# Moving transposes from the matmul engine to DMA in a sorted-attention kernel, with a paired value turn and a new order of the first item

## Chip, cores, metric

One core of one Trainium2 chip. The metric is device microseconds (us) of one execution; lower is better. Engines: PE is the matmul engine (TensorE), PEld its weight load, DVE is VectorE, ACT is ScalarE, POOL is GpSimd, SP issues DMAs.

## The reference

Four batch items, each with 8 heads, 768 positions and 64 dimensions per head, then one feed-forward layer on the joined heads. Inputs and output are float32; the kernel computes in bf16.

```python
def _attn_ref(q, k, v, sort_net):
    P = sort_net                       # (4, 8, 8, 8): per head an 8x8 matrix
    for _ in range(5):                 # exp, then rows and columns normalised
        P = np.exp(P - np.max(P, axis=-1, keepdims=True))
        P = P / (np.sum(P, axis=-1, keepdims=True) + 1e-09)
        P = P / (np.sum(P, axis=-2, keepdims=True) + 1e-09)
    # blocks of 96 positions are mixed by P ("sorted")
    k_sorted = np.einsum('bhij,bhjcd->bhicd', P, k_b)
    v_sorted = np.einsum('bhij,bhjcd->bhicd', P, v_b)
    # softmax attention inside each block: q block i with k_sorted, v_sorted block i
    ...
def _moe_ref(x, w1, w2, w_out):        # x: 3072 x 512, w1 and w2: 512 x 1024
    return np.maximum(x @ w1, x @ w2) @ w_out
```

Since max(h1, h2) = relu(h1 - h2) + h2, the kernel computes h with w1 - w2 ("w_difference") and adds x @ (w2 @ w_out) by a product "wc" formed once.

## The kernel before, in the parts that matter

PSUM is the memory in which PE leaves its results; an "eviction" is the copy out of it by ACT or DVE (1.01 and 1.22 us for 128x1024 elements), which frees the buffer. All PSUM tiles, whatever their name, come from one pool with four buffers.

```python
psum = ctx.enter_context(tc.tile_pool(name="psum", bufs=4, ...))
def ps_f32(name): return psum.tile([128, 1024], FP32, tag="ps", name=name)

def keep_streaming(ps, n, by=None):        # filler matmuls of zeros, n columns
    w0 = fill[:, 0:128] if by is None else late[by]
    while n > 0:
        w = min(n, 512)
        nc.tensor.matmul(ps[:, 0:w], w0, fill[:, 0:w], start=True, stop=True)
        n -= w

def turn_v(rows, eng, c0, c1):             # v from (position, dim) to (dim, position)
    dst = v_dc[rows, 0 : D * BLK].rearrange("p (d c) -> p d c", c=BLK)[:, :, c0:c1]
    src = v_raw[rows].rearrange("p (c d) -> p d c", d=D)[:, :, c0:c1]
    # ACT: nc.scalar.copy, DVE: nc.vector.tensor_copy

def q_transposes(b, half, eng=None):       # ... allocates qT[b] when half == 0
    ps = ps_bf16("tq_ps")
    for n in range(2 * R):                 # R = 6
        if b in q_pair:                    # two heads side by side: one matmul for both
            nc.tensor.matmul(ps[:, c], q_pair[b][:, hp, r], ident, is_transpose=True, ...)
            continue
        for h2 in range(2):                # else one matmul per head
            nc.tensor.matmul(ps[h2 * 64 : ..., c], q_raw[b][:, hp + 4 * h2, ...], ident,
                             is_transpose=True, ...)
    evac(qT[b][...], ps[...], ...)         # eviction on ACT or DVE

def sort_v(b, t, n=0, eng=None):           # 16 matmuls, weights from v_dc (dense columns)
    ps = ps_f32("v_ps")
    keep_streaming(ps, n)
    for m in range(16):
        d = t * 16 + m
        nc.tensor.matmul(..., v_dc[r0 : r0 + 64, d * BLK : d * BLK + 128], bd_v[b][...], ...)
    evac(...)

def x_transposes(b, t, eng=None):          # 8 matmuls and an eviction with re-ordering
    ps = ps_bf16("tx_ps")
    x = x_tiles.pop((b, ih, hh))
    for m in range(8): nc.tensor.matmul(..., is_transpose=True, ...)
    evac(xT[...], ps..., 2 * TCH, eng=eng)
```

While item b runs through the layer (its "units": eight h units of 1.3 us, then output products), the attention of item b + 1 is prepared between the units. The preparation is a list of **steps**. The loop spreads them evenly by their count. SC is a score group (PE, then an exponential on ACT), VA a values group, TR an x transpose, ks and vs key and value sorts, qs the two q transpose halves.

```python
for b in range(B):
    ...
    if b == 0:
        steps = group(*vs[:3]) + qs[:1] + group(*SC[0:2], vs[3]) + qs[1:] + VA[:1]
        steps += group(*SC[2:5]) + VA[1:2]
    elif b == 1: ...                        # pair_q, key sorts, q, scores, value sorts
    else: ...
    steps += VA[2:3] + TR[:1] + VA[3:4]
    steps += group(*rest[:-1]) + TR[1:2] + VA[4:5] + rest[-1:] + VA[5:6]
    done = 0
    for n, unit in enumerate(units):
        unit()
        for step in tail.get(n, []): step()          # fixed places
        total = sum(cost[lo:-2])
        want = -(-len(steps) * sum(cost[lo : n + 1]) // total)   # by count of steps
        while done < min(want, len(steps)):
            steps[done](); done += 1
    tail = {0: [VA[6]], 1: [TR[2], VA[7]], 2: [TR[3]]}
```

The softmax here doesn't subtract the row's maximum and nothing guards it: scores larger than these inputs give would overflow.

## Time and profile before

| | before |
|---|---|
| time, median of 4 runs | 181.78 us (181.24 to 182.06) |
| span of the profiled run | 179.5 us |
| PE busy | 170.0 us, 95% of the span |
| DVE, ACT busy | 94.0 us, 91.8 us |
| clock granted to PE | 1.00 |

The views that carry the argument (busy shares, stretches, chain, waits in the timeline) are quoted in the prediction. Three rows of the groups are added here. Their columns: line, engine, operation, output<-input, shapes, count, then total busy us and the mean ns of one, then idle time before.

```profile
L209 DVE COPY v_dc<-v_raw 64x1536 bf16<-64x1536 bf16 x4 | 5.8, 1492 | 0.0
L207 ACT COPY v_dc<-v_raw 64x1152 bf16<-64x1152 bf16 x1 | 2.2, 2158 | 0.0
L392 PEld LDWEIGHTS <-v_dc 64*128 64x128 bf16 x128 | 4.1, 95 | 1.1 <-issue 0.9
```

A turn of v costs 1492 ns on DVE for 1536 elements, 2158 ns on ACT for 1152; a value weight load costs 95 ns.

### The profile page before, as it was taken

Reading aid. Unit: us, or ns where it says so; the run is one execution under the profiler, and the core shown is the slowest. Engines: PE = TensorE matmul, PEld = TensorE weight load, DVE = VectorE, ACT = ScalarE, POOL = GpSimd, SP = SyncE. Lnnn points to the kernel's source line nnn. Section 1 sums busy time; section 2 is a strip of 40 time slices with the busy share of each in tenths; the row PEclk is TensorE's granted clock in tenths of the full one; section 3 lists DMA queues with packets and bytes.
Section 4 is the critical chain, followed back from the end, with each engine's and each line's share of the span. In section 5 each row is a group of like instructions: output and inputs, shape, how many; then the busy total and the mean of one; then the engine's idle time right before and its main releaser. Section 6 shows DMA issues by size and latency. Waiting matters only on the chain.

```text
span 179.5 us, 4648 instructions
## 1 busy us (share of the span) xinstructions
PE 170.0 (95%) x2083; PEld 100.7 (56%) x2083; DVE 94.0 (52%) x192; ACT 91.8 (51%) x110; POOL 22.9 (13%) x39
## 2 busy tenths in 40 slices
PE   7797989999999989999989999999999999999993
PEld 2246666666565535577655554657555546554453
DVE  5878498559864395253586436156245415340210
ACT  3695876777664445368784341465833233520021
POOL 7861443200180000001000000000000000000000
PEclk9999999999999999999999999999999999999999
DMA  3999999999299991235600113200001132000333
GB/s 58 201 204 206 200 207 214 194 202 208 55 120 221 206 250 48 99 117 74 108 4 0 57 63 117 104 17 5 0 4 42 74 117 116 4 0 4 117 117 117
DMA packets 13939, 19.17 MB, mean 107 GB/s; under 512 B 800, under 2 KB 8864, under 8 KB 13920
## 3 DMA queue, kind: packets, MB, share of 16 engines
q0 software_dynamic: 10304, 12.58, 41.6%
q1 hardware_dynamic: 3328, 6.10, 8.9%
q8 instruction: 16, 0.26, 0.6%
q10 hardware_dynamic: 288, 0.20, 0.3%
q14 instruction: 3, 0.02, 0.0%
HBM read 25.17 MB, written 6.29 MB: 175 GB/s over the span
## 4 chain that ended last, share of the span: by engine, by line
PE 58%; DMA 29%; DVE 5%; issue 4%; POOL 2%; ACT 1%; POOLq 0%; DVEq 0%
PE out_ps L590 32%; PE h_ps L563 16%; DMA v_raw<-in_v_dram 10%; DMA w_sb<-in_moe_w_dram 10%; DMA q_raw<-in_q_dram 9%; PE o_ps L463 3%; PE tx_ps L495 2%; PE k_ps L371 2%; PE s_ps L438 2%; DVE g L579 2%; PE tq_ps L341 1%; DVE x L480 1%; DVE xT L105 1%; POOL v_raw L153 1%; DVE v_dc L209 1%
## 5 line engine op out<-in xcount | busy, mean ns | idle before, releaser
L590 PE MATMUL out_ps<-wo_sb,g 128*128 128x512 bf16 (+2 forms) x208 | 48.1, 363 | 0.2 <-DVE g L579 0.2
L563 PE MATMUL h_ps<-xT,w_sb 128*128 128x384 bf16 x256 | 46.1, 326 | 0.5 <-DVE g L579 0.2
L563 PEld LDWEIGHTS <-w_sb 128*128 128x128 bf16 x256 | 23.6, 97 | 15.1 <-issue 0.7
L577 ACT ACTIVATE g<-h_ps 128x768 bf16<-128x768 f32 x24 | 19.4, 811 | 23.4 <-PE h_ps L563 23.4
L446 ACT ACTIVATE e<-s_ps 96x768 bf16<-96x768 f32 x32 | 24.1, 804 | 14.0 <-PE s_ps L438 13.9
L590 PEld LDWEIGHTS <-g 128*128 128x128 bf16 x208 | 17.7, 97 | 15.8 <-issue 0.2
L590 PE MATMUL out_ps<-wc,xT 128*128 128x512 bf16 (+2 forms) x104 | 25.0, 362 | 0.0
L103 ACT COPY o<-out_ps 128x1024 f32<-128x1024 f32 x8 | 8.1, 1012 | 31.0 <-PE out_ps L590 27.3
L480 DVE TENSOR_TENSOR x<-o_ps,rs 96x512 bf16<-96x512 f32 x32 | 22.0, 687 | 1.1
L474 DVE RECIPROCAL rs<-o_ps 96x8 f32<-96x8 f32 x32 | 6.4, 201 | 27.4 <-PE o_ps L463 27.2
L590 PEld LDWEIGHTS <-xT 128*128 128x128 bf16 x104 | 9.9, 98 | 10.9
L209 DVE COPY v_dc<-v_raw 64x1536 bf16<-64x1536 bf16 (+2 forms) x9 | 14.1, 1583 | 1.8 <-DMA v_raw<-in_v_dram 1.7
L463 PEld LDWEIGHTS <-e 96*128 96x128 bf16 x256 | 11.2, 98 | 6.5 <-DVE x L480 1.1
L579 DVE TENSOR_SCALAR g<-h_ps 128x768 bf16<-128x768 f32 x8 | 7.7, 958 | 13.5 <-PE h_ps L563 10.6
L463 PE MATMUL o_ps<-v_sb,e 96*128 96x65 bf16 x256 | 12.9, 193 | 1.3 <-DVE x L480 0.6
L105 DVE CAST v_sb<-v_ps 96x1024 bf16<-96x1024 f32 x7 | 8.5, 1217 | 5.9 <-PE v_ps L392 3.9
L103 ACT CAST v_sb<-v_ps 96x1024 bf16<-96x1024 f32 x9 | 8.7, 1010 | 3.4 <-PE v_ps L392 2.6
L103 ACT CAST kT<-k_ps 128x1024 bf16<-128x1024 f32 x10 | 9.5, 1024 | 0.0
L103 ACT COPY xT<-tx_ps 128x768 bf16<-128x768 bf16 x11 | 8.8, 797 | 1.5 <-PE tx_ps L495 1.5
L438 PEld LDWEIGHTS <-kT 64*128 64x128 bf16 x256 | 6.2, 94 | 5.4 <-issue 4.4
L129 POOL DMA_DIRECT2D q_raw<-in_q_dram x4 | 3.6, 901 | 43.0 <-DVE q_pair L326 40.7
L438 PE MATMUL s_ps<-qT,kT 64*128 64x96 bf16 x256 | 9.0, 204 | 0.1
(78 smaller groups left out, 162.5 us busy)
## 6 DMA issues: line engine op xcount, KB each, us to landing
out_dram<-o SPq DMA_DIRECT2D x11, 512.0 KB, 2.8
k_raw<-in_k_dram POOLq DMA_DIRECT2D x12, 256.0 KB, 13.7
q_raw<-in_q_dram POOLq DMA_DIRECT2D x4, 768.0 KB, 8.9
v_raw<-in_v_dram POOLq DMA_DIRECT2D x6, 384.0 KB, 12.0
w_sb<-in_moe_w_dram POOLq DMA_DIRECT2D x3, 512.0 KB, 15.7
wo_sb<-in_moe_w_out_dram POOLq DMA_DIRECT2D x2, 512.0 KB, 19.9
v_raw<-in_v_dram POOLq DMA_DIRECT2D x3, 256.0 KB, 5.1
w_sb<-in_moe_w_dram POOLq DMA_DIRECT2D x2, 256.0 KB, 14.3
```

What stands on the lines that cost most here:

```text
L103: nc.scalar.copy(out=out_ap, in_=in_ap)
L105: nc.vector.tensor_copy(out=out_ap, in_=in_ap)
L209: nc.vector.tensor_copy(out=dst, in_=src)
L438: nc.tensor.matmul(ps[:, h2 * 512 + ii * BLK : h2 * 512 + (ii + 1) * BLK], kT[b][rows, (hp * 8 + i) * BLK : (hp * 8 + i) * BLK + 128], rhs ...
L446: nc.scalar.activation(out=e[:, 0 : 8 * BLK].rearrange("p (t f) -> p t f", t=2), in_=ps[0:BLK].rearrange("p (t f) -> p t f", t=2)[:, :, 0 ...
L463: nc.tensor.matmul(ps[:, h2 * 512 + ii * 65 : h2 * 512 + (ii + 1) * 65], e[:, (h2 * 4 + ii) * BLK : (h2 * 4 + ii) * BLK + 128], v_sb[:, m0 ...
L474: nc.vector.reciprocal(out=rs, in_=ov[:, :, :, 64])
L480: nc.vector.tensor_tensor(out=x, in0=ov[:, :, :, 0:D], in1=rs.to_broadcast([BLK, 2, 4, D]), op=ALU.mult,)
L563: nc.tensor.matmul(h_ps[t][:, m * 512 : m * 512 + TCH], w1_sb[:, hp, fb * 128 : (fb + 1) * 128], xT[:, b % 2, ch, hp % 2, hp // 2, :], sta ...
L577: nc.scalar.activation(out=g, in_=src, func=AF.Relu)
L579: nc.vector.tensor_scalar(out=g, in0=src, scalar1=0.0, scalar2=None, op0=ALU.max)
L590: nc.tensor.matmul(dst, g_tiles[b, ch, m // 2][:, m % 2, off : off + 128] if m < NFB else xT[:, b % 2, ch, hp % 2, hp // 2, off : off + 12 ...
```

## The change

Its intent is to take work off PE, which sets the time after 40 us. The x transposes of items 2 to 4 and the q transposes of items 3 and 4 become DMA transposes; the q transposes of item 2 stay on PE and lose their pairing. The value turn moves pairs of bf16 as 32-bit words on DVE (and pair by pair on ACT), so that value weights are read with a step of two. The first item is put in another order with far fewer filler matmuls, the opening fillers have 160 columns instead of 512, and the loads are queued in another order. The step lists are adapted: more of each item's x transposes lie in them, and fewer in the fixed places. Not shown in the cut below: the re-ordering of positions moves from the eviction of x to the exponential, the scores take 128 columns each in PSUM, and x gets a fourth buffer.

```diff
-    keep_streaming(ps_f32("fill_ps"), 18 * 512)
+    keep_streaming(ps_f32("fill_ps"), 76 * 160, most=160)
 # turn_v on DVE; on ACT the same pairs as a fourth dimension "two"
+        out=dst.bitcast(U32).rearrange("p (d c) -> p d c", c=BLK)[:, :, c0:c1],
+        in_=src.bitcast(U32).rearrange("p (c d) -> p d c", c=BLK)[:, :, c0:c1],
+    def v_weights(rows, d):
+        c = d // 2 * (2 * BLK) + d % 2
+        return v_dc[rows, c : c + 255 : 2]
 # q_transposes; the paired form on PE goes
+        if b > 1:
+            nc.sync.dma_start_transpose(out=qT[b][:, hps]..., in_=q_pair[b][:, hps]...)
+            return
 # x_transposes
+        if b:
+            nc.sync.dma_start_transpose(out=xT[:, b % 2, ih, hh]..., in_=x...)
+            return
 # first item (cut): order changed, fillers thinned
-    sort_v(0, 0, 256, "A")
-    sort_v(0, 1, 384, "A")
+    sort_v(0, 0, 0, "D")
+    sort_v(0, 1, 0, "A")
 ... (cut: further lines of this kind)
-        8: [pair_q(1, 0), pair_q(1, 1), load_q(2), load_v(2), load_v(3)],
+        9: [load_v(2), load_v(3), load_k(3)],
+        14: [load_q(2)],
+        18: [pair_q(2, 0), pair_q(2, 1), load_q(3)],
             elif b == 1:
-                steps = group(*pairs) + group(*ks) + qs[:1] + group(*SC[0:2], vs[0]) + qs[1:]
-                steps += group(*vs[1:4]) + group(*vs[4:7]) + group(*SC[2:4], vs[7]) + VA[:2]
+                tail[1] = qs
+                steps = group(*ks) + group(*vs[0:3]) + group(*vs[3:6]) + group(*vs[6:8])
+                steps += group(*SC[0:2]) + group(*SC[2:4]) + VA[:2]
             else:
-                steps = group(*pairs) + group(*ks) + qs + group(*SC[0:2])
+                tail[1] = qs
+                tail[4] = ks
+                steps = group(*SC[0:2]) + group(*SC[2:5]) + VA[:2]
+                lo = 6
 # all items
             steps += group(*rest[:-1]) + TR[1:2] + VA[4:5] + rest[-1:] + VA[5:6]
+            steps += TR[2:3] + VA[6:7]
-        tail = {0: [VA[6]], 1: [TR[2], VA[7]], 2: [TR[3]]}
+        tail = {0: [VA[7], TR[3]]}
```

More of the change, by code (lines that the diff above doesn't have):

```diff
@@ L12 @@
 BF16 = mybir.dt.bfloat16
+U32 = mybir.dt.uint32
 @with_exitstack
@@ L74, with keep_streaming @@
     late = {}
-    def keep_streaming(ps, n, by=None):
+    def keep_streaming(ps, n, by=None, most=512):
         w0 = fill[:, 0:128] if by is None else late[by]
         while n > 0:
-            w = min(n, 512)
+            w = min(n, most)
             nc.tensor.matmul(ps[:, 0:w], w0, fill[:, 0:w], start=True, stop=True)
@@ L118 @@
         nc.vector.memset(kT[b][:, 32 * BLK :], 0.0)
-    v_dc = big.tile([128, D * BLK + 32], BF16, tag="v_dc", name="v_dc")
+    v_dc = big.tile([128, D * BLK + 64], BF16, tag="v_dc", name="v_dc")
     nc.vector.memset(v_dc[:, D * BLK :], 0.0)
@@ L203, in turn_v @@
     def turn_v(rows, eng, c0, c1):
-        dst = v_dc[rows, 0 : D * BLK].rearrange("p (d c) -> p d c", c=BLK)[:, :, c0:c1]
-        src = v_raw[rows].rearrange("p (c d) -> p d c", d=D)[:, :, c0:c1]
+        dst, src = v_dc[rows, 0 : D * BLK], v_raw[rows]
         if eng == "A":
-            nc.scalar.copy(out=dst, in_=src)
-        else:
-            nc.vector.tensor_copy(out=dst, in_=src)
+            nc.scalar.copy(
+                out=dst.rearrange("p (d c two) -> p d c two", c=BLK, two=2)[:, :, c0:c1],
+                in_=src.rearrange("p (c d two) -> p d c two", c=BLK, two=2)[:, :, c0:c1],
+            )
+        else:
+            nc.vector.tensor_copy(
+                out=dst.bitcast(U32).rearrange("p (d c) -> p d c", c=BLK)[:, :, c0:c1],
+                in_=src.bitcast(U32).rearrange("p (c d) -> p d c", c=BLK)[:, :, c0:c1],
+            )
+    def v_weights(rows, d):
+        c = d // 2 * (2 * BLK) + d % 2
+        return v_dc[rows, c : c + 255 : 2]
     rowsum = const.tile([G, NB], FP32, tag="rowsum", name="rowsum")
@@ L335, in q_transposes @@
             qT[b] = qpool.tile([128, HP, R, 128], BF16, tag="qT", name="qT")
+        if b > 1:
+            hps = slice(half * 2, half * 2 + 2)
+            nc.sync.dma_start_transpose(
+                out=qT[b][:, hps].rearrange("p h r c -> p (h r) c"),
+                in_=q_pair[b][:, hps].rearrange("p h r d -> p (h r d)"),
+            )
+            return
         ps = ps_bf16("tq_ps")
@@ L339, in q_transposes @@
             c = slice(n * 128, (n + 1) * 128)
-            if b in q_pair:
-                nc.tensor.matmul(
-                    ps[:, c], q_pair[b][:, hp, r], ident, is_transpose=True, start=True, stop=True
-                )
-                continue
             for h2 in range(2):
@@ L393, in sort_v @@
                 ps[:, m * 64 : (m + 1) * 64],
-                v_dc[r0 : r0 + 64, d * BLK : d * BLK + 128],
+                v_weights(slice(r0, r0 + 64), d),
                 bd_v[b][r0 : r0 + 64, :],
@@ L414, in sort_v_pair @@
                     ps[:, par * 512 + m * 64 : par * 512 + (m + 1) * 64],
-                    v_dc[rows, d * BLK : d * BLK + 128],
+                    v_weights(rows, d),
                     bd_v[b][rows, :],
@@ L438, in scores @@
                 nc.tensor.matmul(
-                    ps[:, h2 * 512 + ii * BLK : h2 * 512 + (ii + 1) * BLK],
+                    ps[:, h2 * 512 + ii * 128 : h2 * 512 + ii * 128 + BLK],
                     kT[b][rows, (hp * 8 + i) * BLK : (hp * 8 + i) * BLK + 128],
@@ L446, in scores @@
         nc.scalar.activation(
-            out=e[:, 0 : 8 * BLK].rearrange("p (t f) -> p t f", t=2),
-            in_=ps[0:BLK].rearrange("p (t f) -> p t f", t=2)[:, :, 0 : 4 * BLK],
+            out=e[:, 0 : 8 * BLK].rearrange("p (t c r) -> p t c r", t=8, r=R),
+            in_=ps[0:BLK]
+            .rearrange("p (t f) -> p t f", t=8)[:, :, 0:BLK]
+            .rearrange("p t (r c) -> p t c r", r=R),
             func=AF.Exp,
@@ L476, in values @@
             x_tiles[b, ih, hp // 2] = xpool.tile(
-                [BLK, 2, 4, 2, D], BF16, tag="x", name="x", bufs=3
+                [BLK, 2, 4, 2, D], BF16, tag="x", name="x", bufs=4
             )
@@ L490, in x_transposes @@
         ih, hh = divmod(t, 2)
+        x = x_tiles.pop((b, ih, hh))
+        if b:
+            nc.sync.dma_start_transpose(
+                out=xT[:, b % 2, ih, hh].rearrange("p h (i c) -> p (h i) c", c=BLK),
+                in_=x.rearrange("p t i n d -> p (t i n d)"),
+            )
+            return
         ps = ps_bf16("tx_ps")
-        x = x_tiles.pop((b, ih, hh))
         for m in range(8):
@@ L495, in x_transposes @@
             nc.tensor.matmul(
-                ps[:, h2 * 1024 + ii * BLK : h2 * 1024 + (ii + 1) * BLK],
+                ps[:, m * BLK : (m + 1) * BLK],
                 x[:, h2, ii].rearrange("p n d -> p (n d)"),
@@ L502, in x_transposes @@
             )
-        dst = xT[:, b % 2, ih, hh].rearrange("p h (i c r) -> p h i c r", r=R, c=PB)
-        src = ps.rearrange("p (h f) -> p h f", h=2)[:, :, 0:TCH].rearrange(
-            "p h (i r c) -> p h i c r", r=R, c=PB
+        evac(
+            xT[:, b % 2, ih, hh].rearrange("p h f -> p (h f)"),
+            ps[:, 0 : 2 * TCH],
+            2 * TCH,
+            two_x=True,
+            eng=eng,
         )
-        evac(dst, src, 2 * TCH, eng=eng)
     w2T = big.tile([128, NFB, DMODEL], BF16, tag="w2T", name="w2T")
@@ L647 @@
             selections(0)
-            turn_v(first, "A", 0, 11)
+            turn_v(first, "A", 0, 18)
         if it == 3:
-            turn_v(first, "A", 11, 22)
-    turn_v(first, "A", 22, 40)
+            turn_v(first, "A", 18, 36)
+    turn_v(first, "A", 36, 56)
+    turn_v(first, "A", 56, 80)
     block_diagonals(0)
-    turn_v(first, "D", 56, 96)
-    turn_v(first, "A", 40, 56)
+    turn_v(first, "D", 80, 96)
     SC, VA, TR = att(0)
     sort_k(0, 0, 2048, "A")
-    sort_k(0, 1, 512, "A")
-    sort_k(0, 2, 256, "D")
+    sort_k(0, 1, 256, "D")
+    sort_k(0, 2, 256, "A")
+    sort_v(0, 0, 0, "D")
+    sort_v(0, 1, 0, "A")
     q_transposes(0, 0, "D")
-    sort_v(0, 0, 256, "A")
-    sort_v(0, 1, 384, "A")
-    sort_v(0, 2, 384, "D")
-    sort_v(0, 3, 384, "A")
+    sort_v(0, 2, 0, "A")
+    scores(0, 0)
+    sort_v(0, 3, 0, "D")
+    scores(0, 1)
     q_transposes(0, 1, "D")
-    scores(0, 0, 256)
-    scores(0, 1, 256)
-    values(0, 0, 512)
+    values(0, 0)
     SC[2]()
+    VA[1]()
     SC[3]()
-    VA[1]()
-    values(0, 2, 512)
+    values(0, 2, 256)
     x_transposes(0, 0, "A")
@@ L675 @@
     SC[4]()
-    moe_h_products(0, 0, 0, (0, 2), 512)
+    moe_h_products(0, 0, 0, (0, 2), 256)
     x_transposes(0, 1, "A")
@@ L691, in turn @@
         turn_v(rows, "D", c0, c0 + 24)
-        load["D"] += 1600
+        load["D"] += 850
     def load_rest():
@@ L706 @@
         7: [lambda: turn(second, 72)],
-        8: [
-            lambda: pair_q(1, 0),
-            lambda: pair_q(1, 1),
-            lambda: load_q(2),
-            lambda: load_v(2),
-            lambda: load_v(3),
-        ],
+        9: [lambda: load_v(2), lambda: load_v(3), lambda: load_k(3)],
+        14: [lambda: load_q(2)],
+        18: [lambda: pair_q(2, 0), lambda: pair_q(2, 1), lambda: load_q(3)],
     }
@@ L738 @@
             qs = [lambda half=half: q_transposes(b + 1, half) for half in range(2)]
-            pairs = [lambda two=two: pair_q(b + 1, two) for two in range(2)]
             ks = [lambda t=t, b=b: sort_k(b + 1, t) for t in range(3)]
@@ L755 @@
                 vs = [lambda t=t: sort_v_pair(2, t) for t in range(8)]
-                steps = group(*pairs) + group(*ks) + qs[:1] + group(*SC[0:2], vs[0]) + qs[1:]
-                steps += group(*vs[1:4]) + group(*vs[4:7]) + group(*SC[2:4], vs[7]) + VA[:2]
-            else:
-                steps = group(*pairs) + group(*ks) + qs + group(*SC[0:2])
-                steps += group(*SC[2:5]) + VA[:2]
+                tail[1] = qs
+                tail[10] = [lambda: pair_q(3, 0), lambda: pair_q(3, 1)]
+                steps = group(*ks) + group(*vs[0:3]) + group(*vs[3:6]) + group(*vs[6:8])
+                steps += group(*SC[0:2]) + group(*SC[2:4]) + VA[:2]
+            else:
+                tail[1] = qs
+                tail[4] = ks
+                steps = group(*SC[0:2]) + group(*SC[2:5]) + VA[:2]
+                lo = 6
             rest = SC[4:] if b == 1 else SC[5:]
@@ L773 @@
                 done += 1
-        tail = {0: [VA[6]], 1: [TR[2], VA[7]], 2: [TR[3]]}
-        if b == 0:
-            tail[3] = [lambda: load_k(3)]
-            tail[8] = [lambda: load_q(3)]
+        tail = {0: [VA[7], TR[3]]}
 _INS = ['q', 'k', 'v', 'sort_net', 'moe_w1', 'moe_w2', 'moe_w_out']
```

## The prediction

> **What bounds the kernel now.** I read the page's busy shares first, then busy time by stretches, then the chain that ended last, then the timeline of its weak places.
>
> ```profile
> PE 170.0 (95%) x2083; PEld 100.7 (56%) x2083; DVE 94.0 (52%) x192; ACT 91.8 (51%) x110; POOL 22.9 (13%) x39
> ...
> 70.00:80.00 10.00, 10.00 (x87) 5.58 (x85) 4.78 (x10) 4.74 (x6) 0.00 (x0) 1.00 0.28 106
> 80.00:90.00 10.00, 9.85 (x197) 7.15 (x194) 4.97 (x7) 7.69 (x10) 0.90 (x1) 1.00 0.58 82
> ...
> 100.00:110.00 10.00, 10.00 (x101) 5.23 (x100) 4.10 (x7) 4.59 (x6) 0.00 (x0) 1.00 0.18 68
> ```
>
> In the stretches (start:end, length, then busy time of PE, weight loads, DVE, ACT and POOL, then clock, DMA share and GB/s) PE is full from about 40 us to 177 us, while DVE and ACT are half used. So from 40 us on, time on PE is time of the kernel, and DVE or ACT time is worth something only where PE waits for it. The chain gives what each kind of PE work costs there, overlap taken out:
>
> ```profile
> 80.38 0.34 PE tx_ps L495 x8
> 80.72 1.64 PE k_ps L371 x96
> 82.36 1.41 PE h_ps L563 x8
> 83.76 0.67 PE tq_ps L341 x12
> 84.43 1.31 PE h_ps L563 x8
> ```
>
> A group of eight x transposes costs 0.34 us and a half of an item's paired q transposes 0.67 us, though the groups list 0.2 us for each single matmul: those durations overlap. The waits that remain on PE after 40 us are few. Two, in the timeline:
>
> ```profile
> 64.39 0.42 PE L463 MATMUL o_ps<-v_sb,e 96*128 96x65 bf16 x8 [0.60 <-DVE x L480]
> ...
> 154.10 0.51 PE L495 MATMUL tx_ps<-ident,x 96*128 96x96 bf16 x8 [0.34 <-DVE x L480]
> ```
>
> The 0.60 us goes back to DVE idling 1.72 us for v_raw, whose load stood in the POOL queue behind a q load that waited for pair_q. The 0.34 us at 154 us is the end of an item, where the last x must be normalised before it is transposed; there is another such at 118.5 us. Waits for a PSUM buffer that DVE still evicts come to 0.24, 0.24 and 0.26 us (91, 94 and 130 us). In all about 2.0 us.
>
> Before 40 us the start is set by latencies and by the loads, which run at 200 GB/s or more in every slice to 45 us:
>
> ```profile
> 27.31 0.67 DVE L190 TENSOR_TENSOR w_sb<-w_sb 128x1024 bf16<-128x1024 bf16 x1
> 28.66 1.23 DVE L105 COPY w2T<-tw_ps 128x2048 bf16<-128x2048 bf16 x1 [0.68 <-PE tw_ps L518]
> 29.81 0.68 DVE L190 TENSOR_TENSOR w_sb<-w_sb 128x1024 bf16<-128x1024 bf16 x1
> ```
>
> The weight difference at 27.31 us starts just as the last w1 piece lands (27.17 us by the chain). That landing does not move with this change, so a faster attention before it is worth only what lies after it: the 0.68 us for which DVE then waits for PE.
>
> [...] The trace fits a cost by element: turns of 2560 and 1536 elements took 2.38 and 1.49 us, so 0.87 ns per element and 0.16 us fixed; 768 words should take 0.83 us. [...] The paired layout makes the value weights step by two; the present loads are all dense (16 loads with their matmuls in about 0.5 us), so no run here shows it yet. [...] The trace has no transposing DMA. Its plain 512 KB stores land 2.8 us after issue[...].
>
> **The change part by part.**
>
> x transposes of items 2 to 4 (b = 1 to 3) leave PE: 12 groups x 0.34 = 4.1 us off the path. Their evictions (about 0.8 us on ACT, 0.95 us on DVE, 12 of them, some 10 us) leave engines that are not the bound. Each becomes one DMA of 96x1024 bf16 = 197 KB[...].
>
> q transposes of items 3 and 4 leave PE: 4 x 0.67 = 2.7 us. Item 2 loses its pairing: 24 instructions instead of 12 per half. Unpaired, the next PE instruction starts 0.79 us later (20.00 to 20.79), paired 0.68 us (49.46 to 50.14), so +0.1 x 2 = +0.2 us. The DMA of a half is 393 KB[...]; they are issued after the second unit of an item and first used some 8 to 9 us later (five h units of 1.3 us plus the key sort of 1.64 us). [...]
>
> Load order: both value loads now stand ahead of the q load, and the first half of v_raw is free from 13 us on. They should land near 53 us in place of 61.9, ahead of the first two-item turn. That ends the 0.60 us wait.
>
> Paired turn: four turns of 1.48 us at 41 to 47 us and four of 1.48 us at 62 to 72 us become 0.83 us each: 5 us off DVE, none of it directly on the path; it helps the three buffer waits. On ACT the present turn costs (2158-1384)/(1152-704) = 1.73 ns per element, twice DVE's; if one access fetches a pair it becomes about 0.87, and 18 columns (1152 elements) take 1.2 us, inside the space of 1.6 us that ACT has between two exponentials.
>
> First item: without most of the filler matmuls, and with value sorts ahead of the q that arrives at 15.9 us, my replay of the new order with the old durations puts the first h product at 24.0 us in place of 25.9. Then DVE waits for the w1 piece at 27.2 us and goes on without a gap: difference 0.68, eviction 1.2, difference 0.68, normalising 0.9, so the third h unit at 30.8 us in place of 31.8. I take -0.8 us. The 160-column fillers at the beginning run longer, but end near 8.6 us, beside the normalisation steps that set the time until 11.3 us: no change.
>
> Item ends: the 0.34 us waits at 118 and 154 us go, as no PE transpose waits for x. In their place the first h unit of the second half (the fifth unit) waits for the last x's DMA. From the end of its values group there are three h units, 3.9 us, plus 0.3 us as the late half is used second; normalising takes 1.1 us of it. That leaves 3.1 us for a transfer[...]. For item 2 the last q load is in flight then, so I put 0.5 us of waiting there and 0.2 us for each of the other two.
>
> Third item's preparation: six sorts now follow one unit without an h unit between them, with four PSUM buffers. Evictions of about 1 us on two engines need some 7 us for 7.8 us of PE work. I allow 0.4 us of new waits and count the old buffer waits (0.7 us) as only half gone.
>
> Sum: -4.1 - 2.7 + 0.2 - 0.6 - 0.7 (item ends) - 0.35 - 0.8 + 0.9 + 0.4 = -7.8 us, so 174.0. The waits on DMA are the softest term; without them it is 172.7. I choose 173.6 us, 4.5% below 181.78.
>
> **The rivals.**
>
> First: the transposes by DMA are late. For it: [...]the issuing queue is shared in order with the output stores, and the last q load is in flight at the first item end. Against it: the DMA share falls to 0.14 to 0.28 from 100 us on, and the third x transposes of an item were moved earlier, as by someone who knows the latency. At 5 us each[...] it costs about 2 us at three item ends, and 1 to 2 us before the scores of items 3 and 4: 179 to 181 us.
>
> Second: strided value weights load slower. If a load takes twice as long, 128 loads after 40 us for the paired items and 64 for item 2 cost 15 to 30 ns more each, 3 to 4 us: 177 us. [...]
>
> Third: the transposes are hidden anyway, as PE work moved elsewhere. I give it little: the chain from 40 us on is PE from instruction to instruction, and DVE and ACT have half their time free, so no other engine takes over at once. It would leave only the start and the load order, 180 us.
>
> Fourth, upward: the head gains the whole 2 us (if the w1 piece is not what holds it) and no DMA is waited for: 171 us.
>
> **Range and chances.** The removed PE work, 6.8 us, is the firm part; the rivals can each take back 2 to 5 us, and I think neither likely nor both at once. Range 170.8 to 177.6 us. The 2% limit lies at 178.1 us, so faster 0.90, same 0.08, slower 0.02.
>
> **What would show it right or wrong.** Right: PE's instruction count falls by 96 + 48 and rises by 24 for the transposes (fillers apart), PE busy stays at 95% or above, the stretches from 40 us on stay full, no wait of PE for DMA exceeds 0.5 us, turns of 768 words take 0.83 us, and the third h unit begins near 30.8 us. Wrong: PE waiting for xT or qT behind a DMA, the value sorts taking over 0.5 us per 16, ACT turns above 1.6 us that hold up the exponentials, or DVE and ACT evictions showing up as releasers of PE in the third item's preparation. If issue to landing of an x transpose is above 3.1 us, my term for the item ends is too small.

## The result and the profile after

Ratios in this document are the mean time of one kernel's fast runs over the mean of the fast runs of the kernel before in the same rounds, so they are not quite the ratio of the medians quoted.

| | before | after |
|---|---|---|
| median of 4 runs | 181.78 us (181.24 to 182.06) | 178.19 us (176.69 to 179.71) |
| the runs of after | | 176.84, 179.54 (slow), 176.69, 179.71 (slow) |
| ratio of fast runs, 95% | | 0.972 (0.970 to 0.975) |
| span, profiled run (fast) | 179.5 us | 175.0 us |
| PE busy | 170.0 us | 162.3 us |

The change is faster, by 2.8% in its fast runs. Two of its four runs were slow, which the kernel before almost never shows (1 of 33 runs). This is a second finding beside the size of the gain; both are followed below. The first page line of after is this:

```profile
PE 162.3 (93%) x1999; PEld 99.8 (57%) x2014; DVE 83.1 (47%) x186; ACT 79.9 (46%) x98; POOL 22.9 (13%) x39
```

PE lost 7.7 us of busy time, DVE 10.9 and ACT 11.9. But the span lost only 4.5: PE's busy share *fell* from 95% to 93%. The groups that answer to those shown of before:

```profile
L212 DVE COPY v_dc<-v_raw 64x768 uint32<-64x768 uint32 x4 | 3.2, 834 | 0.0
L207 ACT COPY v_dc<-v_raw 64x1152 bf16<-64x1152 bf16 x2 | 2.4, 1176 | 0.0
L404 PEld LDWEIGHTS <-v_dc 64*128 64x128 bf16 x128 | 4.0, 95 | 0.6 <-issue 0.4
```

The turn went from 1492 to 834 ns on DVE, so a word takes about as long as a single bf16 element did, which the prediction had assumed and the trace of before does not show; on ACT it went from 2158 to 1176 ns (in pairs 1536 elements take 1511 ns, so 0.87 ns per element). A weight load with a step of two still takes 95 ns. The DMA issues (output<-input, issuing engine, count, then median us from issue to landing):

```profile
xT<-x SPq DMA_TRANSPOSE x12, 3.5
qT<-q_pair SPq DMA_TRANSPOSE x4, 4.1
```

The quickest x took 2.8 us for its 197 KB, the quickest q 3.6 us for 393 KB; the median of x is above the 3.1 us that the prediction had left for it at the item ends. The same three stretches as in the prediction:

```profile
70.00:80.00 10.00, 9.95 (x155) 6.04 (x153) 1.78 (x4) 4.01 (x5) 0.00 (x0) 1.00 1.11 205
80.00:90.00 10.00, 8.90 (x197) 5.73 (x192) 5.75 (x6) 8.64 (x11) 0.00 (x0) 1.00 0.63 100
...
100.00:110.00 10.00, 9.95 (x74) 4.88 (x74) 2.67 (x6) 2.95 (x4) 0.00 (x0) 1.00 0.52 144
```

From 80 to 90 us PE now stands for 1.1 us of ten. The waits of PE after 40 us (who waited <- for what: us in total, times, longest) say for what:

```profile
PE h_ps L585 <- DMA xT<-x: 0.8, 1, 0.8
PE out_ps L612 <- DVE o L106: 0.7, 1, 0.7
PE o_ps L477 <- ACT e L458: 0.6, 1, 0.6
PE out_ps L612 <- ACT o L104: 0.5, 1, 0.5
PE h_ps L585 <- ACT kT L104: 0.5, 1, 0.5
PE v_ps L425 <- ACT kT L104: 0.5, 1, 0.5
PE h_ps L585 <- ACT e L458: 0.4, 1, 0.4
...
```

Five more lines of 0.2 to 0.3 us follow. One wait is for a DMA (0.76 us). The others are 4.5 us together, of which 0.3 us are put down to issue. The remaining 4.2 us, nine waits, are of one kind: a PE group needs a PSUM buffer, and ACT or DVE has not yet emptied one. Before, waits of that kind were 0.74 us after 40 us, and all waits together about 2.0.

The spans can be cut at the same PE work in each timeline. "Paced" is an experiment described below; it differs from after only in the spreading of the steps.

| stretch of PE work | before | after | paced |
|---|---|---|---|
| start to the key sort of item 2 | 42.76 | 41.47 | 42.01 |
| to the first h product of item 2 | 32.72 | 32.75 | 31.79 |
| to the first h product of item 3 | 37.82 | 36.33 | 35.08 |
| to the first h product of item 4 | 35.56 | 33.76 | 32.34 |
| to the end | 30.65 | 30.72 | 30.72 |
| span | 179.51 | 175.03 | 171.94 |

In these traces the first item's new order gave 1.3 us, the stretches to the h products of items 3 and 4 gave 1.5 and 1.8; the second and the last stretch gave nothing. The first stretch is the least steady: paced leaves it as it is in after, and over six traces of that same start it is 41.21 to 42.01.

### The profile page after: what moved, and what is told of

It is laid out like the page before. It is cut to its first block, busy times and chain, and to the rows that moved or that the text cites. A ratio compares the mean times of both kernels' runs of the same rounds, so it can differ in the third digit from the quotient of the medians.

```text
span 175.0 us, 4519 instructions
## 1 busy us (share of the span) xinstructions
PE 162.3 (93%) x1999; PEld 99.8 (57%) x2014; DVE 83.1 (47%) x186; ACT 79.9 (46%) x98; POOL 22.9 (13%) x39
## 4 chain that ended last, share of the span: by engine, by line
PE 73%; DMA 9%; ACT 6%; issue 5%; DVE 2%; POOL 2%; ACTq 0%; DVEq 0%; POOLq 0%
PE out_ps L612 33%; PE h_ps L585 23%; DMA q_raw<-in_q_dram 7%; PE wc_ps L563 4%; PE o_ps L477 3%; PE k_ps L383 3%; ACT e L458 3%; PE s_ps L450 2%; DMA xT<-x 2%; ACT g L599 2%; PE tq_ps L358 1%; PE v_ps L404 1%; DVE qT L106 1%; PE tw_ps L540 1%; POOL k_raw L145 1%
## 5 line engine op out<-in xcount | busy, mean ns | idle before, releaser
L612 PE MATMUL out_ps<-wo_sb,g 128*128 128x512 bf16 (+2 forms) x198 | 46.2, 362 | 1.8 <-DVE o L106 0.7
L585 PE MATMUL h_ps<-xT,w_sb 128*128 128x384 bf16 x256 | 45.2, 326 | 1.9 <-DMA xT<-x 0.8
L599 ACT ACTIVATE g<-h_ps 128x768 bf16<-128x768 f32 x23 | 18.6, 812 | 18.1 <-PE h_ps L585 18.1
L601 DVE TENSOR_SCALAR g<-h_ps 128x768 bf16<-128x768 f32 x9 | 8.6, 957 | 18.2 <-PE h_ps L585 18.2
L612 PEld LDWEIGHTS <-xT 128*128 128x128 bf16 x104 | 9.9, 98 | 10.9
L106 DVE CAST v_sb<-v_ps 96x1024 bf16<-96x1024 f32 x8 | 9.7, 1217 | 8.0 <-PE v_ps L425 5.1
L104 ACT CAST kT<-k_ps 128x1024 bf16<-128x1024 f32 x9 | 8.8, 1016 | 3.0 <-PE k_ps L383 3.0
L104 ACT CAST v_sb<-v_ps 96x1024 bf16<-96x1024 f32 x8 | 7.9, 1012 | 3.8 <-PE v_ps L404 3.7
L82 PEld LDWEIGHTS <-fill 128*128 128x128 bf16 x84 | 8.7, 123 | 1.7 <-DVE fill L73 1.2
L82 PE MATMUL fill_ps<-fill 128*128 128x160 bf16 x76 | 8.2, 292 | 1.2 <-DVE fill L73 1.2
L106 DVE COPY o<-out_ps 128x1024 f32<-128x1024 f32 x3 | 3.7, 1225 | 9.3 <-PE out_ps L612 9.3
```

Of the source, the lines that this page charges most:

```text
L104: nc.scalar.copy(out=out_ap, in_=in_ap)
L106: nc.vector.tensor_copy(out=out_ap, in_=in_ap)
L585: nc.tensor.matmul(h_ps[t][:, m * 512 : m * 512 + TCH], w1_sb[:, hp, fb * 128 : (fb + 1) * 128], xT[:, b % 2, ch, hp % 2, hp // 2, :], sta ...
L599: nc.scalar.activation(out=g, in_=src, func=AF.Relu)
L601: nc.vector.tensor_scalar(out=g, in0=src, scalar1=0.0, scalar2=None, op0=ALU.max)
L612: nc.tensor.matmul(dst, g_tiles[b, ch, m // 2][:, m % 2, off : off + 128] if m < NFB else xT[:, b % 2, ch, hp % 2, hp // 2, off : off + 12 ...
```

## The experiments

The granted clock of each run (the share of full speed at which PE was allowed to run) is recorded. Some runs counted as fast have 0.99; such a run of after takes some 1 to 3 us longer. So beside the ratios I give means of runs with a clock of at least 0.997 ("full clock"). They are pooled from three chips and the first four runs, whose chip is not recorded; the kernel before has 181.82 us there (32 of its 33 runs), and its medians on the three chips are 181.73, 181.82 and 181.88. After, with its own repetition, has 177.17 (6 of 10 runs). Full-clock runs of one kernel still spread by up to 1.4 us (paced: 172.65 to 174.02), so a mean of two of them is good to some 0.5 us only, by my estimate. All kernels below gave correct results.

| run | what it is | ratio to before, 95% | full clock: mean us (runs) | runs below full clock |
|---|---|---|---|---|
| again | after itself | 0.978 (0.975 to 0.981) | 177.38 (4) | 2 of 6 |
| x_pe | after, x transposes back on PE | 1.014 (1.011 to 1.017) | 183.78 (4) | 2 of 6 |
| q_pe | after, q transposes back on PE | 0.978 (0.975 to 0.980) | 177.70 (3) | 3 of 6 |
| early | after, last values and x step moved ahead | 0.967 (0.964 to 0.970) | 175.45 (4) | 2 of 6 |
| paced | after, fewer steps for the same work | 0.956 (0.952 to 0.960) | 173.47 (4) | 2 of 6 |
| x_fair | paced, x on PE, apart | 0.980 (0.978 to 0.983) | 177.62 (2) | 4 of 6 |
| paced_q | paced, q on PE | 0.962 (0.958 to 0.965) | 174.36 (2) | 4 of 6 |
| fillers | after, fillers of the first item restored | 0.973 (0.971 to 0.974) | 176.91 (5) | 0 of 5 |
| fill512 | after, opening fillers as before | 0.975 (0.971 to 0.979) | 175.93 (1) | 5 of 6 |
| best160 | paced + early + fillers | 0.960 (0.959 to 0.962) | 174.58 (4) | 0 of 4 |
| best512 | best160, opening as before | 0.958 (0.957 to 0.960) | 174.26 (4) | 0 of 4 |
| b_turn | before, with the paired turn alone | 0.993 (0.992 to 0.995) | 180.64 (6) | 0 of 6 |

After my reading of the two traces I held this **theory**: the operations give what I predicted, but the step lists place them so densely that PE waits for PSUM buffers. The **rivals**: the DMA transposes are late and cost the difference; or the removed transposes were worth less than their durations said.

### again: how steady is after?

No edit.

> The changed kernel itself, for the same chip and more runs: fast runs 176.5 to 177, slow runs near 179.6 with a clock of 0.97 to 0.99 in 2 to 4 of 6.

Measured: 177.61 us median, 177.16 to 179.04, ratio 0.978. The full-clock runs, 177.16 to 177.71, lie above the 176.5 to 177 that I expected. Two of six runs had a lower clock (0.99). So the slow runs belong to this kernel, and the gain lies between 2 and 3% according to how many of them a set of runs holds.

### x_pe and q_pe: the transposes back on PE

```diff
 # x_pe, in x_transposes              # q_pe, in q_transposes
-        if b:                        -        if b > 1:
+        if False:                    +        if False:
                                      +            (the paired matmuls of before)
```

> The changed kernel with one thing undone: the x transposes of items 2 to 4 are on PE again (12 groups of eight, 0.34 us each in the trace of before). My theory (the transposes were on the path, and part of what they freed came back as waits for PSUM buffers and one wait for a DMA of 0.8 us): 12 x 0.34 = 4.1 us more, less the DMA wait of about 0.9 us, plus up to 1 us of new buffer waits, so 179.5 to 181 against 176.8 (fast runs). Rival 'the x DMAs are late': 176 to 178, since their waits go too. Rival 'transposes were hidden anyway': about 177.

> The changed kernel with the q transposes of items 3 and 4 on PE again, at the same places in the program (4 halves at 0.67 us). Theory: +2.7 us, so 179.2 to 180 against 176.8. Rival 'hidden anyway': 176.5 to 177.5. Rival 'q DMAs are late or hold up the x DMAs behind them': below 178.5.

Both missed, in opposite directions. **x_pe** took 183.8 us, 6.6 above after where I expected some 3. Its waits show why:

```profile
PE tx_ps L515 <- DVE x L494: 4.4, 4, 1.7
```

The new lists put the last values group and the last x transpose back to back, which a DMA does not mind, since PE goes on (in after PE waits 0.76 us in all for an x DMA). A PE transpose there waits for the normalisation on DVE: 4.4 us at four places. With 4.1 for the transposes, less 0.8 each for the DMA wait that goes and for PSUM waits (3.4 in place of 4.2), this makes 6.9; the two spans differ by 7.0. The experiment thus measured a bad place, not the operation.

**q_pe** took only 0.5 us more at full clock (177.70 against 177.17), where the removed work counts 2.7. In its trace the preparation of item 4 is 1.35 us longer, as it should be. That of item 3 is only 0.79 us longer, since the two waits of 0.51 us for the kT eviction shrink to one of 0.18: the transposes fill that time. And in item 4 the last x DMA is no longer late (paced_q below shows why). Part of the freed time had therefore been given back in waits. Whether the q DMA is worth more in a better schedule is asked again in paced_q.

### paced: the same operations, fewer steps

A DMA transpose has no instruction on PE (in the trace its lines, L507 and L348, are on the queue of SP alone), but each is a step of its own in the lists, and the count decides the spread. For item 2's preparation the list grew from 15 to 17 steps over the same units, so every piece of real work falls earlier and closer to the next. For item 3 it has 18 steps as before, for item 4 14 in place of 16, but over four units fewer. Paced has 15, 15 and 11. Here each such transpose is grouped with the values group beside it. No operation is added or removed.

```diff
-            steps += VA[2:3] + TR[:1] + VA[3:4]
-            steps += group(*rest[:-1]) + TR[1:2] + VA[4:5] + rest[-1:] + VA[5:6]
-            steps += TR[2:3] + VA[6:7]
+            steps += VA[2:3] + TR[:1] + VA[3:4] if b == 0 else group(VA[2], TR[0]) + VA[3:4]
+            steps += group(*rest[:-1]) + group(TR[1], VA[4]) + rest[-1:] + VA[5:6]
+            steps += group(TR[2], VA[6])
```

> The changed kernel with another pacing only: the DMA transposes, which cost PE nothing, no longer count as steps of the schedule but ride with a values group (for item 2 all but the first), so that score groups and sorts are spread over more units and none falls where an output tile turns over. No operation is added or removed. Theory (about 3 us of the missing gain are waits of PE for PSUM buffers behind evictions and exponentials: 0.33 and 0.16 and 0.62 us near 55 us, 0.51 and 0.51 near 82, 0.53 at 99, 0.28 and 0.35 and 0.35 near 123, 0.68 at 133): 174 to 175 against 176.8, and those waits mostly gone from the trace. Rivals 'late DMAs' or 'slow strided weights': unchanged, 176.5 to 177.

Measured: 173.47 us at full clock, 3.7 below after, a little more than I expected. Ratio 0.956. The waits of PE after 40 us, whole:

```profile
PE h_ps L585 <- DMA xT<-x: 0.7, 1, 0.7
PE h_ps L585 <- DVE g L601: 0.2, 1, 0.2
PE out_ps L612 <- DVE g L601: 0.2, 1, 0.2
PE out_ps L612 <- issue: 0.2, 1, 0.2
```

The PSUM waits fell from 4.2 to 0.4 us; the DMA wait stayed. Two places show how it works. The timeline of PE in after (start, us, operation, count, then in brackets the idle time before and what ended it):

```profile
56.27 0.68 PE L450 MATMUL s_ps<-qT,kT 64*128 64x96 bf16 x24
57.57 0.40 PE L477 MATMUL o_ps<-v_sb,e 96*128 96x65 bf16 x8 [0.62 <-ACT e L458]
...
97.86 0.68 PE L450 MATMUL s_ps<-qT,kT 64*128 64x96 bf16 x24
99.08 1.89 PE L612 MATMUL out_ps<-wo_sb,g 128*128 128x512 bf16 x7 [0.53 <-ACT o L104]
```

And in paced:

```profile
56.52 0.69 PE L450 MATMUL s_ps<-qT,kT 64*128 64x96 bf16 x24
57.14 0.60 PE L612 MATMUL out_ps<-wo_sb,g 128*128 128x512 bf16 x2
...
98.07 0.68 PE L450 MATMUL s_ps<-qT,kT 64*128 64x96 bf16 x24
98.68 0.61 PE L612 MATMUL out_ps<-wo_sb,g 128*128 128x512 bf16 x2
```

Three score groups take three of the four PSUM buffers; the output tile being filled holds the fourth. In after the next thing at 57.57 us is a values group. It needs a buffer and waits until an exponential (about 0.8 us each on ACT) has emptied one. In paced, output products that go into the buffer already held come first. At 97.86 us in after the score groups fall exactly where the output tile turns over, so the next output product needs a new buffer while the eviction of the old one (1.0 us on ACT) is under way. In paced the same scores fall two products before the end of a tile. This settles the theory against the first rival: nothing but the places changed, and 3.7 us of the missing gain came back. The traces agree: from the key sort of item 2 to the last matmul PE takes 130.18 us in after and 126.49 in paced, 3.69 less, and its waits there are 3.9 us less. (The spans differ by 3.1 only, for the starts differ by 0.5.)

### early: the last values and x step ahead

```diff
-            steps += TR[2:3] + VA[6:7]
+            steps += TR[2:3] + VA[6:7] + group(VA[7], TR[3])
-        tail = {0: [VA[7], TR[3]]}
+        tail = {}
```

> The changed kernel with the last values group and the last x transpose of each item moved from after the first unit of the next item into the end of the step list; all else stays. Theory: only the wait of 0.76 us [...] for the last item's x goes, so 175.8 to 176.3 against 176.8, partly eaten by a denser step list. Rival 'late DMAs are where the missing gain went': 174 or below.

Measured: 175.45 us, 1.7 below after, slightly more than expected. The DMA wait of 0.76 us is gone, and so is a PSUM wait of 0.7 us at 133 us, which I had not counted on; but two others of 0.41 us each came, at 56 and 63 us. Another 0.5 us of the difference lies after the last eviction (see paced_q). So the late DMA is worth little more than the time of its one wait, not the difference of 3 us that the first rival needed.

### x_fair: what the x DMAs are worth in a good order

Paced with x on PE, where the last x transpose stands one unit behind its values group as in the kernel before.

```diff
 # against paced
-        if b:                                 # x_transposes
+        if False:
-        tail = {0: [VA[7], TR[3]]}
+        tail = {0: [VA[7]], 1: [TR[3]]}
-                tail[1] = qs                  # twice
+                tail[1] += qs
```

> The paced kernel with the x transposes of items 2 to 4 back on PE, and with one unit between the last values of an item and their transpose, as the kernel before had it (the first try, x_pe, had none, and PE waited 4.4 us for x there). Theory (12 x 0.34 = 4.1 us of PE work on the path, plus two waits of 0.34 us, less the DMA wait of 0.7 us): 3.5 to 4.5 us above paced, so 177 to 178.3 against 173.6 in fast runs. Rival 'transposes on PE were hidden': 174 or below. Rival 'they cost the 7.3 us that x_pe showed': 180.5 or above.

Measured: 177.62 us (2 full-clock runs) against 173.47, so 4.15 us, in the middle of what I expected. The traces say the same: from the key sort of item 2 to the last matmul x_fair takes 4.48 us more than paced, of which 0.44 are waits. The rest, 4.04 us, is the predicted count of 12 groups at 0.34 us.

### paced_q: what the q DMAs are worth in a good order

The q_pe edit on paced.

> The paced kernel with the q transposes of items 3 and 4 on PE (4 x 0.67 us). In the changed kernel the same step cost only 0.9 us in fast runs. Theory (there the freed PE time of item 3 fell into PSUM waits of the sorts that replaced it, and the q transposes do no harm to the x ones): with the waits spread, about 2.7 us less the DMA wait of 0.7 us if that goes, so 175.4 to 176.4 against 173.5 in runs with a full clock. Rival (q by DMA is worth only 0.9 us in any schedule): 174 to 174.6.

Measured: 174.36 us (2 full-clock runs) against 173.47: 0.9 us, not the 2 to 3 that my theory expected. The rival of this run, "0.9 in any schedule", gave the right number, but the trace shows another reason. (Its profile fell into a slow run, but the clock is full after 32 us, and only what comes later is used here.) The preparations of items 3 and 4 are 1.24 and 1.34 us longer, which is the 2.6 us of removed transposes, as predicted. But the last stretch is 1.23 us *shorter*. Of this, 0.87 us is the wait for the last x, which is not late in this kernel, with what follows from it; the other 0.36 us lies after the last eviction, while the last stores land. Here is item 4's last x transpose in paced, a DMA view of 143 to 149 us in slices of 0.15 us:

```profile
GB/s 0 0 109 396 410 355 382 396 423 369 369 273 123 0 90 150 155 159 191 109 5 7 10 9 10 10 241 165 0 0 0 0 0 0 0 0 0 0 0 0
...
q8 instruction: 1, 0.02, 1.2%
...
xT<-x SPq DMA_TRANSPOSE x1, 3.9
```

And in fill512 (after with 58 fewer matmuls in the opening, see below), 149.80 to 155.80 us:

```profile
GB/s 0 0 0 300 410 396 355 382 410 396 341 410 96 0 24 162 164 160 179 266 253 101 2 0 0 0 0 0 0 0 0 0 0 0 0 0 0 0 0 0
...
xT<-x SPq DMA_TRANSPOSE x1, 2.8
```

The first hump is a store of output, the second the transpose. In paced the transfer falls to 5 to 10 GB/s for about 1 us before its last part lands, and a 16 KB fetch of instructions (queue q8; the 16 in the trace of after took 0.9 to 1.4 us each) falls just there. In q_pe, paced_q and fill512 no fetch falls there, and the transpose lands after 2.8 us; in after, again, paced and fillers one does, and it lands after 3.8 to 4.0 us. Fill512 comes near to an experiment on this: it differs from after in the opening matmuls alone, so that the fetches fall elsewhere; PE does not wait for the last x, and the work from the first h product of item 4 to the last matmul takes 26.41 us in place of 27.34. It is one profile, of a slow run whose clock is full again after 30 us, and the fetch was not its purpose. The last stores tell the same tale: in after, again and paced a fetch falls beside them, and 3.05 to 3.65 us pass between the last eviction and the end; in q_pe, paced_q and fill512, without one, it is 2.6 to 2.7 (but fillers has one too and takes 2.56, so a fetch there does not always cost). So the 0.9 us is no measure of what the q transposes are worth on PE: they show their 2.6 us, and some 1.2 us of that is hidden by where fetches happen to fall. The remaining 0.5 us lies in the start and the spread of two to four runs.

### fillers and fill512: where the slow runs come from

Fillers restores the zero matmuls of the first item to the amounts of before; fill512 restores the opening.

```diff
 # fillers (cut)
-    sort_v(0, 0, 0, "D")
-    sort_v(0, 1, 0, "A")
+    sort_v(0, 0, 256, "D")
+    sort_v(0, 1, 384, "A")
 ...
-    moe_h_products(0, 0, 0, (0, 2), 256)
+    moe_h_products(0, 0, 0, (0, 2), 512)
 # fill512
-    keep_streaming(ps_f32("fill_ps"), 76 * 160, most=160)
+    keep_streaming(ps_f32("fill_ps"), 18 * 512)
```

> The changed kernel with the zero matmuls inside the first item put back to the amounts of before (256 to 512 columns ahead of sorts, scores and values), the 160-column ones at the start kept. Theory on the slow runs (clock 0.99 or 0.971: one or three clock windows of 3.41 us at half rate, because PE is too little busy in the first item): no slow run in 6, and fast runs within 0.5 us of 176.8, as PE waits there anyway. Rival (slow runs come from the 160-column matmuls at the start, or by chance): about 2 of 6 slow again.

> The changed kernel with the opening zero matmuls as before: 18 of 512 columns in place of 76 of 160. In the profiled run of the changed kernel these ended at 9.4 us and pushed the first useful matmul from 11.35 to 11.9 us. Theory: fast runs 0 to 0.5 us faster than 176.8 (176.3 to 176.8), and slow runs as often as with the changed kernel, since the low activity lies later. Rival (the 160-column matmuls cause the slow runs): no slow run in 6. Rival (they protect the clock): more slow runs, 4 or more of 6.

**Fillers**: 176.91 us in five runs, all at clock 1.0. So in the time of the whole run the fillers cost nothing that shows (after has 177.17 at full clock), and the slow runs are gone. Its trace is less simple: the key sort of item 2 starts at 42.34 us, 0.9 later than in after and 0.6 later than in again, and the time after the last eviction is 0.5 to 1.1 us shorter (2.56). **Fill512**: the single full-clock run had 175.93 us, too few to state a gain (its trace has the two fetches out of the way, as shown above, which would be some 1.4 us); five of six runs were below full clock, and its profile fell into such a run. The clock row of its page, 40 slices of 4.4 us, shows where:

```profile
PEclk9999756999999999999999999999999999999999
```

Two stretches there (start:end, length, PE, PEld, DVE, ACT, POOL busy, clock, DMA share, GB/s):

```profile
16.17:19.58 3.41, 1.65 (x52) 1.38 (x47) 1.48 (x2) 2.49 (x3) 0.27 (x1) 1.00 1.37 200
19.58:23.00 3.42, 2.88 (x48) 2.40 (x47) 2.04 (x2) 0.81 (x1) 2.93 (x3) 0.50 1.28 205
```

The same stretch in fillers, with the clock full before and after:

```profile
16.17:19.58 3.41, 3.09 (x73) 2.28 (x70) 1.82 (x2) 1.91 (x2) 0.54 (x1) 1.00 1.36 199
```

The clock is halved (0.50) in pieces of 3.41 us: for three of them in this run (19.6 to 29.8 us), for one in the profiled run of x_fair (23.8 to 27.2 us). A mean clock of 0.97 is three such pieces, 0.99 one. PE was busy for 1.65 us (48%) of the 3.41 us before the drop here, and for 2.48 us (73%) in x_fair; with the fillers it is 3.1 and 2.9 us in the stretches of that length from 16.17 and 19.58 us. The longest gap of PE before the drop was 1.51 us in fill512 and 0.48 us in x_fair. What decides I cannot say, as one such stretch of the kernel before (12.76 to 16.17 us) had only 2.44 us of PE work and kept its clock; where no drop shows, the trace does not tell where such a piece would begin.

Over all runs: of 52 runs of kernels with thinned fillers 26 were below full clock; of 13 with the fillers restored none; of b_turn, which has the first item of before, 0 of 6; of before 1 of 33. That the thinned fillers cause the slow runs is shown by the exchange.

### best160 and best512: everything together

> The paced kernel, with the last values group and x transpose of an item moved into the end of its steps (as in early), and with the zero matmuls inside the first item put back (as in fillers). Theory: 173.5 - 0.7 to 0.9 for the last x, fillers free, so 172.3 to 173, and every run with a clock of 0.998 or more. If the fillers cost time once the rest is faster: 173.5 or above.

> As best160, with the opening zero matmuls also as before (18 of 512 columns). Theory (these end earlier[...]): 0.3 to 1 us below best160, so 171.5 to 172.7, no slow run as the fillers of the first item are there. Rival (the 160-column matmuls are what keeps the clock up): slow runs in half, as fill512 had with the fillers taken out.

The edits are those of paced, early and fillers; best512 also has the opening of before.

```diff
+            steps += group(TR[2], VA[6]) + group(VA[7], TR[3])      # on top of paced
+        tail = {}
```

Measured: 174.58 and 174.26 us, with all eight runs at full clock. Both missed my expectation by 1.5 us or more: the combination is 1.1 us *slower* than paced at full clock. The trace of best160 shows the mechanism once more. Early adds one step to the list, everything falls closer together, and the PSUM waits come back: 0.33 us at 52.9 us for an exponential, 0.60 at 85.7, 0.56 at 100.7 and 0.43 at 125.0 us. Gains of placing don't add. Best512 is 0.3 us below best160; the intervals of the two ratios overlap, so this is not settled. For an engineer who wants the best average, best512 is the fastest that was measured with no slow run in it: 4.2% below before. Paced with the fillers alone was not run; from paced and fillers I estimate about 173.5 us in every run.

### b_turn: the paired turn alone

The kernel before, with the paired turn_v and v_weights of the change and nothing else.

> The kernel before with the paired value turn alone (same columns on the same engines). Theory: turns of 768 words take 0.83 us in place of 1.48, about 5 us off DVE, none of it on the path except the one turn behind the v load at 62 us (0.60 us wait of PE) and perhaps a buffer wait: 181.0 to 181.6 against 181.8. Rival (DVE time counts in full): 177. Rival (strided weight loads are slow): above 182.5.

Measured: 180.64 us, 1.2 below before, so somewhat more than expected. The trace has 0.77 us of the gain at one place, between 42.6 and 74.6 us. There the wait of PE at 64 us, which the prediction had traced to the v load, is gone: pair_q and, after it, the q and v loads started earlier, as the turns ahead of them on DVE were shorter. The other saved DVE time is worth nothing that shows. The load order of the change was not run by itself, so of this wait's end in after I can say only that the paired turn alone suffices.

## Why the prediction was right, and where not

The direction and the bound were right: PE set the time, work taken off it was time gained. The full-clock value is 177.2 us, so 3.6 above the point of 173.6: of the 8.2 us foretold, 4.6 came. The fast runs of the first four (mean 176.77) lie inside the range; their median with the slow ones, 178.19, lies above its top. Of the signs that I had named as right, the turns of 0.83 us and the third h unit near 30.8 us came, while PE at 95%, full stretches and no DMA wait above 0.5 us did not; and evictions as releasers of PE in the third item's preparation, named as a sign of being wrong, came. Two sums in the prediction are off: without the DMA waits its terms give 173.1, not 172.7 (which leaves out the PSUM waits too), and 192 slower loads at 15 to 30 ns make 2.9 to 5.8 us, not 3 to 4. By the terms of the sum:

- **x transposes, -4.1.** Right. x_fair against paced shows 4.15 us, waits included.
- **q transposes, -2.7 + 0.2.** The removed time is right (2.6 us in the two preparations by paced_q; an unpaired half takes 0.80 us, 48.16 to 48.96). The net by the times is 0.9 us. Some 1.2 us of the shortfall goes with the fetches beside the last transfers (paced_q), which the sum could not have; in after, item 3 gives back another 0.5 us in PSUM waits.
- **v load -0.6, item ends -0.7, old buffer waits -0.35.** The first two waits are gone from after. The third was beside the point, as the next term swallowed it.
- **Start, -0.8.** Mis-sized in the good direction: the key sort of item 2 starts 1.29 us earlier, the third h unit begins at 30.54 us (30.8 predicted, 31.83 before). The path is the predicted one, as far as the trace shows: DVE now waits 0.92 us for the w1 piece and then goes on without the old gap of 0.68. But that wait ends at 27.02 us, where the landing had been at 27.17 and the weight difference had begun at 27.31: the landing moved a little, against what I had written. An exponential on ACT ends within 0.05 us of the same point, so the last link is not certain. Its parts were less good: the first h product came at 24.62 us, not 24.0. "No change" from the 160-column opening was wrong: the 76 matmuls ended at 9.37 us, not 8.6, and the first useful matmul began at 11.90 us instead of 11.35.
- **Waits on DMA, +0.9.** Right in size, wrong in place: I expected 0.5 us for item 2 and 0.2 each for the others; it was 0.76 us in item 4 and none in the others. The term was my own allowance, as the trace of before has no transposing DMA: x took 2.8 to 4.7 us, and one 9.1 with a load in flight. Most of it was hidden, by the slack of 3.1 us and, for the 4.7 us of item 2's last x, by item 3's sorts, which stand in between.
- **New PSUM waits, +0.4. This is the step that failed.** I allowed it for six sorts in a row in the third item. There it is 1.0 us (two waits of 0.51 behind the kT eviction), and 3.1 us more at seven other places, so 4.2 in all in the preparations of three items. I had looked at what was removed and added, item by item, but not at what the new step lists do to the spacing of everything else. Without these waits, in paced, the same operations give 173.47 us against my 173.6. That near agreement is partly luck, since terms above missed both ways.

The rivals. *Late DMA transposes*: by the medians they took 3.5 us for x and 4.1 for q, but PE waited only 0.76 us for them; early and paced speak against more. *Slow strided weights*: false. 95 ns per load before and after, and 48 matmuls of value sorts took 1.51 us before (47.95 to 49.46) and 1.50 after (46.66 to 48.16). *Hidden anyway*: false for x (4.15 us), and for q in the preparations (2.6 us), though only 0.9 us of it came out in the time. *The head gains 2 us*: no, 1.3.

What I did not foresee at all is the clock. I treated the thinned fillers as idle time saved. They saved nothing in the time of the whole run (fillers) and cost half of the runs 1 to 3 us each. Nor did I foresee that some 60 instructions more or less move the fetches, and with them about 1 us.

## What to carry to other kernels

When operations leave the engine that sets the time, count again what is left in the schedule: a step that no longer costs that engine anything should no longer take a slot in its pacing, or the rest crowds together and the gain returns as waits for buffers (here 3.7 of 8 us). Look at places where the number of groups in flight equals the number of buffers, and put work that needs no new buffer there. And read the clock of every run, not only of the one profiled: filler matmuls that look idle may be what holds the clock, and their removal then shows as a slow half of the runs (here 26 of 52, against none of 13 with the fillers restored) rather than in the trace that one reads.
